# A chunked scan and an expert router: the scan rewritten as masked linear attention on small array tiles

## The chip, the cores and the metric

One core of one Trainium2 chip runs the whole program. The metric is the device time of one execution in microseconds. The kernel before takes 391.32 us, the median of 3 runs (389.31 to 393.22).

## What is computed

For 4 batches and 8 heads of 768 tokens (x has 32 columns, B and C have 16), a state decays by `a` at each token. The output of token i is the sum over earlier tokens j of (C_i . B_j), times the product of the decays between them, times x_j. The reference does it in chunks of 32:

```python
L = np.exp(cum[:, :, :, None] - cum[:, :, None, :]) * causal
y_intra = np.einsum('bhij,bhjd->bhid', np.einsum('bhin,bhjn->bhij', Cc, Bc) * L, xc)
y_inter = np.einsum('bhin,bhnd->bhid', Cc, state) * np.exp(cum)[:, :, :, None]
state = decay_full * state + sum_j(B_j x_j * decay_from_j)
```

The outputs of the 8 heads side by side are 3072 rows of 256. Each row goes to the one expert of 8 whose normalised embedding has the largest cosine with it, and the gate is the softmax weight of that expert:

```python
logits = xn @ en.T / tau
out[mask] = gate_w[mask, None] * (np.maximum(x[mask] @ w1[e], 0) @ w2[e])   # w1 256x1024, w2 1024x256
```

All data is f32. On TensorE a product in f32 shows as two records (two weight loads and two matmuls).

## The kernel before

The scan goes in 24 units: 6 chunks of 128 tokens (`c`) times 4 batches (`b`), all 8 heads of a batch in one unit `u`. `decays` loads `a`, clips it, writes it to a scratch tensor `a_dram` in DRAM and makes the running products `prod` (L96). Per unit, `front` reads the decays of the chunk back from `a_dram`, spread over 128 partitions (`row`), and a scan on VectorE (L158) makes from them the triangular decay matrices `L` of the 8 heads; GpSimd makes `bd`, B scaled by the decay to the chunk's end (L164). `inner` makes the scores `g` of four head groups on four row tiles of the array (L182) and VectorE multiplies each into `L` (L183); `dc` (L186) spreads the decays and `cd` (L188) is C scaled by them. `state` makes the chunk's state (L199), VectorE updates it (L208) and GpSimd masks it into `Sm` (L212). `outputs` adds the state's part (L227) and eight products of `L` and x on four column tiles of the array (L233) into `y`, which ScalarE copies to `yT` (L238). `finish` turns it (L248), makes the router's logits (L250), copies both to `yt` (L253), and squares the row (L255).

After each 4 units `place` picks the expert of each row (VectorE), counts with short bf16 products its slot among the expert's rows (L363), and scatters the rows of `yt` to `rows` in DRAM with four indirect DMAs on GpSimd's queue (L371). Slots that get no row were filled with ones by 8 DMAs on ScalarE's queue (L331).

The experts follow in order: `load` reads 416 rows of an expert as 4 x 104 (L396), `turn_x` turns them (L440), `prepare` makes the gates, `up` and `down` are the two products (L449, L463), and `out` turns back, scales (L479) and scatters four blocks (L480). A loop for rows over 416 of an expert closes the program; it goes round as often as there are such blocks, and starts with a load of that number (L584).

All instructions of an engine are in the order that a scheduler chose from the program's order and its own estimates. Each PSUM tile of the scan has a bank of its own.

Of the kernel before, what the change touches and what calls it, by code (L numbers as in the profile page):

```python
# [8 lines left out]
F32 = mybir.dt.float32  # L9
# [15 lines left out]
CAP = TR * NT  # L25
LEFT = (T - CAP) // Q + E
W = DM + E + 2


class Net:  # L30
    pass

# [5 lines left out]
def build_consts(k):  # L38
    nc, pool = k.nc, k.const
    k.ident = pool.tile([128, 128], F32, name="ident")  # L40
    make_identity(nc, k.ident[:])

    k.diag = k.mc.tile([128, NH, Q], F32, name="diag")
    nc.gpsimd.memset(k.diag[:], 0.0)
    nc.gpsimd.affine_select(
        out=k.diag[:], in_=k.diag[:], pattern=[[0, NH], [-1, Q]], compare_op=ALU.not_equal,
        fill=1.0, base=0, channel_multiplier=1,
    )

    k.spread = k.mc.tile([NB * NH, NB, 128], F32, name="spread")  # L50
    nc.gpsimd.memset(k.spread[:], 0.0)
    nc.gpsimd.affine_select(
        out=k.spread[:].rearrange("k b (q t n) -> k (b q) t n", q=4, t=2),
        in_=k.spread[:].rearrange("k b (q t n) -> k (b q) t n", q=4, t=2),
        pattern=[[-8, NB], [-1, 4], [-4, 2], [0, N]], compare_op=ALU.not_equal,
        fill=1.0, base=0, channel_multiplier=1,
    )

    k.tmask = k.mc.tile([128, 2], F32, name="tmask")
    nc.vector.memset(k.tmask[:], 0.0)  # L60
    same = k.work.tile([128, 128], F32, name="same", tag="sq", bufs=1)
    nc.vector.memset(same[:], 0.0)
    for q in range(4):
        nc.vector.memset(k.tmask[32 * q : 32 * q + N, 0:1], 1.0)
        nc.vector.memset(same[32 * q : 32 * q + 32, 32 * q : 32 * q + 32], 1.0)
    nc.vector.tensor_scalar(
        out=k.tmask[:, 1:2], in0=k.tmask[:, 0:1], scalar1=-1.0, scalar2=1.0, op0=ALU.mult, op1=ALU.add
    )
    k.smask = k.mc.tile([128, 2, 128], F32, name="smask")
    for t in range(2):  # L70
        nc.vector.tensor_scalar_mul(k.smask[:, t, :], same[:], k.tmask[:, t : t + 1])
# [6 lines left out]
def decays(k):  # L78

    nc = k.nc
    a = k.work.tile([NB * NH, S], F32, name="a", tag="L", bufs=3)
    nc.sync.dma_start(a[:], k.a.rearrange("b h s -> (b h) s"))
    nc.vector.tensor_scalar(out=a[:], in0=a[:], scalar1=1e-6, scalar2=1.0, op0=ALU.max, op1=ALU.min)
    head = k.work.tile([NB * NH, S], F32, name="head", tag="L", bufs=3)
    nc.vector.memset(head[:], 0.0)
    nc.vector.tensor_copy(out=head[:, 0:S:Q], in_=a[:, 0:S:Q])
    nc.vector.memset(a[:, 0:S:Q], 0.0)
    for b in range(NB):  # L90
        nc.sync.dma_start(
            k.a_dram[b].rearrange("c h s -> h c s"),
            a[NH * b : NH * b + NH, :].rearrange("h (c s) -> h c s", s=Q),
        )
    k.prod = k.mc.tile([NB * NH, S], F32, name="prod")
    nc.vector.tensor_tensor_scan(  # L96
        out=k.prod[:], data0=a[:], data1=head[:], initial=0.0, op0=ALU.mult, op1=ALU.add
    )
    ps = k.ps.tile([128, NB, NC], F32, name="whole_ps", tag="tp")
    for b in range(NB):  # L100
        nc.tensor.matmul(
            ps[:, b, :], lhsT=k.spread[:, b, :], rhs=k.prod[:, Q - 1 : S : Q], start=True, stop=True
        )
    k.whole = k.mc.tile([128, NB, NC], F32, name="whole")
    nc.vector.tensor_copy(out=k.whole[:], in_=ps[:])


def expert_emb(k):

    nc = k.nc  # L110
    emb = k.work.tile([E, DM], F32, name="emb", tag="emb")
    nc.scalar.dma_start(emb[:], k.emb)
    tau = k.mc.tile([E, 1], F32, name="tau")
    nc.scalar.dma_start(tau[:], k.tau.to_broadcast([E, 1]))
    sq = k.work.tile([E, DM], F32, name="emb_sq", tag="sq", bufs=1)
    r = k.mc.tile([E, 1], F32, name="emb_r")
    nc.scalar.activation(sq[:], emb[:], ACT.Square, accum_out=r[:])
# [4 lines left out]
    nc.vector.tensor_scalar_mul(emb[:], emb[:], r[:])  # L122
    ps = k.ps.tile([128, KD, E], F32, name="emb_ps", tag="tp")
    for j in range(KD):
        nc.tensor.transpose(ps[:, j, :], emb[:, 128 * j : 128 * j + 128], k.ident[:E, :E])
    k.en = k.mc.tile([128, KD, E], F32, name="en")
    nc.vector.tensor_copy(out=k.en[:], in_=ps[:])


def load(k, c):  # L130
    nc = k.nc
    t = Net()
    t.bt = k.inp.tile([128, NB, Q], F32, name="bt", tag="bt")
# [15 lines left out]
def front(k, u):  # L149


# [3 lines left out]
    row = k.work.tile([128, NH * Q], F32, name="row", tag="row")  # L155
# [35 lines left out]
def state(k, u):  # L191
# [4 lines left out]
    if c == NC - 1:  # L196
        return
# [495 lines left out]
```

## Time and profile before

| | us |
|---|---|
| median of 3 runs | 391.32 |
| lowest, highest | 389.31, 393.22 |
| the profiled execution | 392.45 |
| its span, first to last instruction | 390.7 |

| engine | busy us | share of the span |
|---|---|---|
| TensorE, matmuls (PE) | 328.1 | 84% |
| TensorE, weight loads (PEld) | 203.0 | 52% |
| VectorE (DVE) | 179.4 | 46% |
| ScalarE (ACT) | 67.8 | 17% |
| GpSimd (POOL) | 119.1 | 30% |

Busy times are shares of the whole span; the scan and the experts have different limits and are read apart, by stretches of time. A line number such as L233 is the line of the kernel that issued an instruction. A matmul's end is modelled, since matmuls overlap; the distance from one group's start to the next group's start is safer than a busy time.

### The profile page before, as it was taken

What the parts mean: (1) busy time and instruction counts of PE and PEld (TensorE: products, weight loads), DVE (VectorE), ACT (ScalarE), POOL (GpSimd) and SP (SyncE); (2) the same over time, 40 slices, a digit from 0 to 9 for tenths busy, and PEclk for the clock granted to TensorE, in tenths of its full rate; (3) what the DMA queues carried; (4) which work ended last, traced back from release to release, by engine and by line L of the source; (5) the groups of instructions that cost most, each with busy time, mean ns of one, the idle gap of its engine ahead of it and who ended that gap; (6) DMA issues with size and microseconds to landing.
All of it is one profiled execution on the core that took longest, in us unless ns stands there. A gap on an engine that the chain in (4) does not pass through costs nothing. (4 is left out here: it accounts for less than half of the span.)

```text
span 390.7 us, 4519 instructions
## 1 busy us (share of the span) xinstructions
PE 328.1 (84%) x1589; PEld 203.0 (52%) x1589; DVE 179.4 (46%) x460; ACT 67.8 (17%) x195; POOL 119.1 (30%) x147
## 2 busy tenths in 40 slices
PE   2319998699999799607999999999999999999940
PEld 2205566477767576504555555555555555555520
DVE  7137876888897968143314225042241412403020
ACT  1101242142333233200101011011110111101100
POOL 7001444527667562243013014140131401304031
PEclk9999996575868669555999999999999999999995
DMA  7978757487847330125044532445324400101010
GB/s 245 298 273 283 253 173 260 163 271 227 289 153 236 120 117 2 56 87 108 6 146 140 160 106 52 143 142 160 107 68 128 144 3 0 39 0 43 0 34 11
DMA packets 24791, 51.23 MB, mean 131 GB/s; under 512 B 2453, under 2 KB 14175, under 8 KB 24768
## 3 DMA queue, kind: packets, MB, share of 16 engines
q1 hardware_dynamic: 21112, 40.97, 33.0%
q0 software_dynamic: 2688, 6.42, 5.2%
q10 hardware_dynamic: 968, 3.55, 2.6%
q8 instruction: 13, 0.21, 0.2%
q14 instruction: 10, 0.08, 0.1%
HBM read 40.87 MB, written 10.32 MB: 131 GB/s over the span
## 5 line engine op out<-in xcount | busy, mean ns | idle before, releaser
L449 PE MATMUL hp<-xT,w 128*128 128x416 f32 x256 | 97.9, 524 | 0.6 <-DVE xT L441 0.6
L463 PE MATMUL yp<-hT,w 128*128 128x416 f32 x256 | 90.8, 513 | 0.0
L463 PEld LDWEIGHTS yp<-hT,w 128*128 128x128 f32 x256 | 48.1, 190 | 38.5 <-issue 38.5
L449 PEld LDWEIGHTS hp<-xT,w 128*128 128x128 f32 x256 | 47.5, 195 | 33.8 <-issue 32.5
L480 POOL DMA_INDIRECT out_dram<-yo,to x32 | 32.2, 1007 | 103.0 <-DVE yo L479 92.3
L158 DVE TENSOR_TENSOR_SCAN L<-row,diag 128x1024 f32<-128x1024 f32 x24 | 56.2, 2341 | 9.9 <-DMA row<-a_dram 6.2
L182 PE MATMUL g<-ctm,bt 32*128 32x256 f32 x192 | 36.9, 586 | 9.9 <-DVE L L183 9.8
L183 DVE TENSOR_TENSOR L<-g,L 128x256 f32<-128x256 f32 x96 | 35.5, 413 | 17.6 <-POOL bd L164 12.3
L455 DVE TENSOR_SCALAR hT<-hp 128x416 f32<-128x416 f32 x32 | 18.9, 592 | 42.4 <-PE hp L449 28.8
L371 POOL DMA_INDIRECT rows<-yt,row_of x24 | 30.4, 1268 | 19.6 <-issue 14.2
L164 POOL TENSOR_TENSOR bd<-b,L 128x64 f32<-128x64 f32 x48 | 17.4, 384 | 54.3 <-DVE L L158 30.7
L453 ACT ACTIVATE hT<-hp 128x416 f32<-128x416 f32 x32 | 16.6, 517 | 91.7 <-PE hp L449 91.7
L212 POOL TENSOR_TENSOR Sm<-S,smask 128x256 f32<-128x256 f32 x20 | 24.1, 1206 | 18.5 <-DVE S L208 11.2
L417 POOL TENSOR_TENSOR gr<-xg,half 104x4 f32<-104x4 f32 x8 | 8.2, 1030 | 70.2 <-DMA xg<-rows 70.2
L182 PEld LDWEIGHTS g<-ctm,bt 32*128 32x128 f32 x192 | 19.1, 250 | 15.8 <-issue 9.8
L470 DVE COPY yoT<-yp 128x416 f32<-128x416 f32 x8 | 4.7, 591 | 43.8 <-PE yp L463 33.2
L178 ACT ACTIVATE ctm<-ct,tmask 128x128 f32<-128x128 f32 x48 | 16.5, 394 | 44.2 <-PE g L182 25.5
L233 PE MATMUL y<-L,x 128*32 128x128 f32 x384 | 23.9, 366 | 0.0
L199 PE MATMUL st<-x,bd 128*128 128x256 f32 x40 | 20.9, 619 | 1.6 <-DVE S L208 1.6
L186 PE MATMUL dc<-prod,spread 32*128 32x128 f32 x48 | 15.8, 423 | 7.6 <-DVE cd L188 7.5
L479 DVE TENSOR_SCALAR yo<-ot,gate 104x256 f32<-104x256 f32 x32 | 15.3, 480 | 11.2 <-PE ot L477 11.2
L411 DVE TENSOR_REDUCE gm<-xg 104x4 f32<-104x32 f32 x8 | 1.5, 184 | 38.3 <-DMA xg<-rows 38.3
(138 smaller groups left out, 283.0 us busy)
## 6 DMA issues: line engine op xcount, KB each, us to landing
w<-in_moe_w_dram SPq DMA_DIRECT2D x16, 1024.0 KB
row<-a_dram SPq DMA_DIRECT2D x24, 512.0 KB
rows<-none ACTq DMA_DIRECT2D x8, 432.2 KB
xg<-rows SPq DMA_DIRECT2D x8, 432.2 KB
x<-in_x_dram SPq DMA_DIRECT2D x6, 512.0 KB
bt<-in_BT_dram SPq DMA_DIRECT2D x6, 256.0 KB
ct<-in_CT_dram SPq DMA_DIRECT2D x6, 256.0 KB
b<-in_B_dram SPq DMA_DIRECT2D x6, 256.0 KB
```

What stands on the lines that cost most here:

```text
L158: nc.vector.tensor_tensor_scan(out=s.L[:].rearrange("j h i -> j (h i)"), data0=row[:], data1=k.diag[:].rearrange("j h i -> j (h i)"), init ...
L164: nc.gpsimd.tensor_tensor(out=s.bd[:, :, v, :], in0=t.b[:, b, :].rearrange("j (q t n) -> j q t n", q=4, t=2)[:, :, v, :], in1=s.L[:, 4 * v ...
L182: nc.tensor.matmul(g[:], lhsT=t.bt[r, b, :], rhs=ctm[r], start=True, stop=True, tile_position=(32 * q, 0))
L183: nc.vector.tensor_tensor(out=s.L[:, q:NH:4, :], in0=g[:], in1=s.L[:, q:NH:4, :], op=ALU.mult)
L199: nc.tensor.matmul(ps[:], lhsT=s.bd[:].rearrange("j q t n -> j (q t n)"), rhs=t.x[:, b, :], start=True, stop=True)
L212: nc.gpsimd.tensor_tensor(out=k.Sm[u][:].rearrange("p t m -> p (t m)"), in0=new[:], in1=k.smask[:].rearrange("p t m -> p (t m)"), op=ALU.mult,
L233: nc.tensor.matmul(y[32 * q : 32 * q + 32, v, :], lhsT=t.x[:, b, D * h : D * h + D], rhs=s.L[:, h, :], start=(c == 0 and v == 0), stop=Tru ...
L371: d = nc.gpsimd.indirect_dma_start(out=k.rows[:, :], out_offset=bass.IndirectOffsetOnAxis(ap=row[:, b : b + 1], axis=0), in_=k.yt[:, NB * ...
L449: nc.tensor.matmul(t[:], lhsT=s.w1[:, j, 128 * f : 128 * f + 128], rhs=s.xT[:, j, :], start=(j == 0), stop=(j == KD - 1))
L455: nc.vector.tensor_scalar_max(s.hT[:, f, :], t[:], 0.0)
L463: nc.tensor.matmul(t[:], lhsT=s.w2[:, f, 128 * j : 128 * j + 128], rhs=s.hT[:, f, :], start=(f == 0), stop=(f == KF - 1),)
L480: d = nc.gpsimd.indirect_dma_start(out=k.out[:, :], out_offset=bass.IndirectOffsetOnAxis(ap=s.to[:, i : i + 1], axis=0), in_=y[:], in_offs ...
```

## The change

The scan is written anew. The decays are taken relative to the middle of each 64 tokens: with f the product of the decays from there (and its inverse r), a score is (C_i f_i) . (B_j r_j) where i >= j, so B and C are scaled once and the decay matrix becomes a mask of ones and zeros. `load_decays`, `decays`, `turn_decays` and `between` make f, r, the turned r, and the factor from one middle to the next; `a_dram` is gone. C comes from DRAM straight into a zeroed tensor in which the even and odd head of a pair have places of their own (8 loads of 32 KB per chunk instead of one). Per unit there are now 64-token halves: `scale_c` (f spread by a product, then C scaled, then scaled B turned by TensorE and copied), `sums` (the halves' states, 8 products on 64x32 tiles), `inner` (8 products on 32x64 tiles, masked in one step on VectorE), `outputs` (16 products of the states on the four diagonal 32x32 tiles, 16 of the masked scores on 64x32 tiles) and `finish` (two products that turn the output and give the logits together). `states` and `scale_b` run once per chunk on VectorE.

PSUM is now four hand-made tensors: pg (4 banks), py (2 banks, outputs and half states), p6 (turned rows, slots and counts) and p7 (spread f and turned B). TensorE's instructions in the scan keep the order in which the program issues them; the other engines' are still scheduled. `place` is split: `pick` (VectorE) and `place`, two iterations later.

Behind the scan: the rows have 272 columns instead of 266 and lie as two halves with the logits between; the squares move from `finish` to `prepare`; an expert's 416 rows are read as 4 rows in a line per partition; only the last 160 of 416 slots are filled with ones; the experts' SBUF pool is opened after the scan's; an order barrier stands ahead of the closing loop.

```diff
+def decays(k, kk):
+    nc = k.nc
+    tt = nc.vector.tensor_tensor
+    a, f, r = k.a0[:, kk, :], k.f[:, kk, :], k.r[:, kk, :]
+    clip(k, a)
...
+    nc.vector.tensor_tensor_scan(out=f, data0=a, data1=k.heads[:], initial=0.0, op0=ALU.mult, op1=ALU.add)
...
+    nc.vector.reciprocal(out=r, in_=f)
+    for v, s in ((r, w[:, 0, :]), (f, w[:, 1, :])):
+        v = v.rearrange("p (h s) -> p h s", h=2)[:, :, 0:SQ]
+        tt(out=v, in0=v, in1=s.unsqueeze(2).to_broadcast([128, 2, SQ]), op=ALU.mult)
+
+def between(k):
...
+    nc.vector.memset(one[:, SQ:S:HQ], 1.0)
+    p = k.mc.tile([NB * NH, S], F32, name="p")
+    nc.vector.tensor_tensor_scan(out=p[:], data0=a[:], data1=one[:], initial=0.0, op0=ALU.mult, op1=ALU.add)
+    k.g = k.mc.tile([NB * NH, NK - 1], F32, name="g")
+    nc.vector.tensor_tensor(out=k.g[:], in0=p[:, HQ + SQ - 1 : S : HQ], in1=at[:, 1:], op=ALU.mult)
+
 def load(k, c):
...
+    t.ct = k.ctz[c % 3]
+    for i in range(8):
+        q, v = divmod(i, 2)
+        r = slice(32 * q + N * v, 32 * q + N * v + N)
+        (nc.scalar if c == 0 and i % 2 else nc.sync).dma_start(
+            t.ct[r, v].rearrange("p b m -> p (b m)"), k.CT[c][r]
+        )
...
+def sums(k, u):
...
+        for q in range(4):
+            nc.tensor.matmul(
+                k.py[32 * q : 32 * q + 32, h, 256 + 64 * b : 320 + 64 * b], lhsT=t.bp[r, b, 32 * q : 32 * q + 32],
+                rhs=t.x[r, b, :].rearrange("p (t q d) -> p q t d", t=2, q=4)[:, q],
+                start=True, stop=True, tile_position=(HQ * h, 32 * q),
+            )
+
+def states(k, c):
+    nc = k.nc
+    for h in range(2):
+        i = (2 * c + h)
+        if i > 0:
+            k.T[i] = k.stp.tile([128, NB, 64], F32, name="T", tag="T", bufs=6)
+            nc.vector.tensor_tensor(
+                out=k.T[i][:], in0=k.V[:], in1=k.whole[:, :, i - 1 : i].to_broadcast([128, NB, 64]), op=ALU.mult
+            )
...
+            nc.vector.tensor_tensor(out=k.V[:], in0=k.T[i][:], in1=s, op=ALU.add)
+
+def scale_c(k, u):
...
+    f = k.p7[:, 128 * (u % 2) : 128 * (u % 2) + 128]
+    nc.tensor.matmul(
+        f, lhsT=k.spread[g : g + 32, b, :], rhs=k.f[g : g + 32, c // 4, :], start=True, stop=True,
+        tile_position=(g, 0),
+    )
+    s.cp = k.work.tile([128, 2, Q], F32, name="cp", tag="cp", bufs=4)
+    nc.vector.tensor_tensor(
+        out=s.cp[:], in0=t.ct[:, :, b, :], in1=f.unsqueeze(1).to_broadcast([128, 2, Q]), op=ALU.mult
+    )
+    bt = k.p7[:, 256 + 128 * (u % 2) : 384 + 128 * (u % 2)]
+    nc.tensor.transpose(bt, t.bp[:, b, :], k.ident[:])
+    s.bt = k.work.tile([128, Q], F32, name="bt", tag="bt", bufs=3)
+    nc.scalar.copy(out=s.bt[:], in_=bt)
 
 def inner(k, u):
...
+    a = 128 * (u % 4)
+    for q in range(4):
+        for h in range(2):
+            r, m = slice(32 * q, 32 * q + 32), slice(HQ * h, HQ * h + HQ)
+            nc.tensor.matmul(
+                k.pg[m, q, a : a + 128], lhsT=s.bt[r, m], rhs=s.cp[r, :, m], start=True, stop=True,
+                tile_position=(32 * q, HQ * h),
+            )
+    s.g = k.work.tile([128, 4, 2, HQ], F32, name="g", tag="g", bufs=3)
+    nc.vector.tensor_tensor(
+        out=s.g[:], in0=k.pg[:, :, a : a + 128].rearrange("p q (t i) -> p q t i", t=2),
+        in1=k.mask[:].unsqueeze(1).unsqueeze(1).to_broadcast([128, 4, 2, HQ]), op=ALU.mult,
+    )
 
 def outputs(k, u):
...
+            for q in range(4):
+                r = slice(32 * q, 32 * q + 32)
+                nc.tensor.matmul(
+                    at(q, h, v), lhsT=T[r, b, 32 * v : 32 * v + 32], rhs=s.cp[r, v, HQ * h : HQ * h + HQ],
+                    start=(v == 0), stop=False, tile_position=(32 * q, 32 * q), skip_group_check=True,
+                )
     for v in range(2):
         for q in range(4):
...
+            for h in range(2):
+                r = slice(HQ * h, HQ * h + HQ)
+                n = 32 * (4 * v + q)
+                nc.tensor.matmul(
+                    at(q, h, v), lhsT=t.x[r, b, n : n + 32], rhs=s.g[r, q, v, :],
+                    start=((2 * c + h) == 0 and v == 0), stop=True, tile_position=(HQ * h, 32 * q),
+                    skip_group_check=True,
+                )
...
 def finish(k, u):
...
+    for j, at in ((0, 0), (1, LG)):
         nc.tensor.matmul(
+            k.p6[:, at : at + Y1], lhsT=yT[:, j].rearrange("p h i -> p (h i)"), rhs=k.turn[:, j, :],
+            start=(j == 0), stop=(j == 1), skip_group_check=True,
+        )
+    nc.scalar.copy(out=k.yt[:, u, 0:TOK], in_=k.p6[:, 0:TOK])
 
 def mamba(k):
...
+    scale_b(k, 0)
+    between(k)
+    for i in range(NU + 3):
+        c, b = divmod(i, NB)
+        if b == 0 and c + 2 < NC:
+            load(k, c + 2)
+        if i in (8, 14, 20):
+            load_weights(k, (i - 8) // 6)
+        if i < NU:
+            scale_c(k, i)
+        if i == 0:
+            spread_between(k)
+            for v in range(NB):
+                sums(k, v)
+        elif NB <= i + 3 < NU:
+            sums(k, i + 3)
...
+        if b == 0 and c < NC:
+            states(k, c)
+            if c + 1 < NC:
+                scale_b(k, c + 1)
+        if 0 <= i - 1 < NU:
+            inner(k, i - 1)
+        if 0 <= i - 2 < NU:
+            outputs(k, i - 2)
+        if 0 <= i - 3 < NU:
+            finish(k, i - 3)
+        if b == 2 and c > 0:
+            pick(k, c - 1)
+        if b == 0 and c > 1:
+            place(k, c - 2)
+    place(k, NC - 1)
...
     def load(s, e):
...
+            s.x[:].rearrange("p t w -> p (t w)"),
+            s.k.rows[T * e : T * e + CAP, :].rearrange("(p t) w -> p (t w)", t=s.nt),
...
     def prepare(s, has):
...
+        for i in range(nt):
+            sq = k.p.tile([tr, 2, 128], F32, name="sq", tag="sq")
+            nc.scalar.activation(
+                sq[:], s.x[:, i, :].rearrange("p (j w) -> p j w", j=KD)[:, :, 0:128], ACT.Square,
+                accum_out=r[:, i : i + 1],
+            )
...
 def leftover(k):
...
+    k.tc.no_sync_barrier()
     blocks = nc.values_load(table[0:1, 1, 0:1], min_val=0, max_val=LEFT)
```

In this, HQ is 64, NK is 12 (the halves), Y1 is 136 and TOK is 264.

## Rows read from the trace of the kernel before

**Rows 1.** The page: the granted clock of PE in 40 slices, tenths.

```profile
PEclk9999996575868669555999999999999999999995
```

**Rows 2.** Busy time by stretch; columns: engines' busy us (records), PEclk, DMA share, GB/s.

```profile
30.00:165.00 135.00, 122.28 (x911) 88.14 (x909) 102.91 (x205) 41.65 (x138) 66.79 (x86) 0.76 0.56 186
...
62.60:83.10 20.50, 17.39 (x107) 12.89 (x107) 14.74 (x23) 4.34 (x14) 10.20 (x12) 0.51 0.63 205
...
205.00:245.00 40.00, 40.00 (x137) 22.10 (x136) 13.88 (x39) 4.87 (x10) 9.14 (x9) 1.00 0.39 120
```

**Rows 3.** Groups by line and shape: busy us, mean ns, idle before and its releaser.

```profile
L158 DVE TENSOR_TENSOR_SCAN L<-row,diag 128x1024 f32<-128x1024 f32 x24 | 56.2, 2341 | 9.9 <-DMA row<-a_dram 6.2 <-PE y L233 3.7
L183 DVE TENSOR_TENSOR L<-g,L 128x256 f32<-128x256 f32 x96 | 35.5, 413 | 17.6 <-POOL bd L164 12.3 <-PE g L182 5.0
L96 DVE TENSOR_TENSOR_SCAN prod<-a,head 32x768 f32<-32x768 f32 x1 | 2.2, 2208 | 0.0
```

**Rows 4.** Tile y: ns of one (least, median, most), first and last start.

```profile
L233 PE MATMUL y<-L,x x384: 272/421/423, 32.6 to 159.5; 128*32 128x128 f32 x192
```

**Rows 5.** PE in order of time, early and late: start us, us, group.

```profile
32.59 1.08 PE L233 MATMUL y<-L,x 128*32 128x128 f32 x16
...
158.79 1.08 PE L233 MATMUL y<-L,x 128*32 128x128 f32 x16
159.81 0.69 PE L248 MATMUL tp<-ident,yT 128*128 128x128 f32 x2
160.29 0.86 PE L250 MATMUL tp<-en,yT 128*128 128x8 f32 x4
```

**Rows 6.** PE in order of time, around 100 us.

```profile
96.39 1.22 PE L199 MATMUL st<-x,bd 128*128 128x256 f32 x2
97.40 1.06 PE L227 MATMUL y<-cd,Sm 128*128 128x128 f32 x4
98.39 1.08 PE L233 MATMUL y<-L,x 128*32 128x128 f32 x16
...
102.54 0.64 PE L233 MATMUL y<-L,x 128*32 128x128 f32 x16
103.11 0.44 PE L248 MATMUL tp<-ident,yT 128*128 128x128 f32 x2
```

**Rows 7.** All engines in order of time: a product, its read, the next.

```profile
12.81 0.79 PE L186 MATMUL dc<-prod,spread 32*128 32x128 f32 x2 [0.38 <-DVE cd L188]
...
13.64 0.29 DVE L188 TENSOR_TENSOR cd<-dc,ct 128x128 f32<-128x128 f32 x1 [0.88 <-PE dc L186]
13.99 0.49 PEld L186 LDWEIGHTS dc<-prod,spread 32*128 32x128 f32 x2 [0.68 <-DVE cd L188]
```

**Rows 8.** The scan's start on DVE, and ACT's longest wait up to 20 us.

```profile
25.86 2.29 DVE L158 TENSOR_TENSOR_SCAN L<-row,diag 128x1024 f32<-128x1024 f32 x1 [4.83 <-DMA row<-a_dram]
28.82 1.42 DVE L183 TENSOR_TENSOR L<-g,L 128x256 f32<-128x256 f32 x4 [0.68 <-POOL bd L164]
...
ACT ctm L178 <- DMA rows<-none: 13.7, 1, 13.7
```

**Rows 9.** The scan's end: last copy of yt, then the slots' records.

```profile
163.37 0.38 ACT L253 COPY yt<-tp 128x264 f32<-128x264 f32 x1 [1.43 <-PE tp L250]
...
164.92 0.18 PE L363 MATMUL at<-ob,before_b 128*128 128x32 bf16 x1 [1.58 <-DVE ob L350]
...
165.19 0.17 PE L382 MATMUL n_ps<-sums,ones_b 128*128 128x8 bf16 x1
```

**Rows 10.** The reload: its issue on SP, first reader, first up-product.

```profile
173.19 6.74 SPq L396 DMA_DIRECT2D xg<-rows  x3
177.83 0.19 DVE L411 TENSOR_REDUCE gm<-xg 104x4 f32<-104x32 f32 x1 [6.55 <-DMA xg<-rows]
...
180.18 13.88 PE L449 MATMUL hp<-xT,w 128*128 128x416 f32 x32 [0.62 <-DVE xT L441]
```

**Rows 11.** The last two scatters, and the closing chain's wait for one.

```profile
378.71 1.00 POOL L480 DMA_INDIRECT out_dram<-yo,to  x1 [0.30 <-POOLq L584]
384.25 1.00 POOL L480 DMA_INDIRECT out_dram<-yo,to  x1 [4.54 <-issue]
...
378.71 3.58 DMA out_dram<-yo,to
```

More of the change, by code (lines that the diff above doesn't have):

```diff
@@ L59, in build_consts @@
[L59 to L68, printed above, removed]
@@ L75, in build_consts, with load_decays @@
     k.yt = pool.tile([128, NU, W], F32, name="yt")
-def decays(k):
+    nc.gpsimd.memset(k.yt[:, :, TOK:], 0.0)
+def load_decays(k):
     nc = k.nc
[L83 to L93, printed above, removed]
-        )
[L95 to L99, printed above, removed]
+    k.a0 = k.mc.tile([128, 2, Q], F32, name="a0")
+    nc.vector.memset(k.a0[64:128, 1, :], 1.0)
+    a = k.a.rearrange("b h s -> (b h) s")
+    for c in range(NC):
+        (nc.sync if c % 2 else nc.scalar).dma_start(
+            k.a0[32 * (c % 4) : 32 * (c % 4) + 32, c // 4, :], a[:, Q * c : Q * c + Q]
+        )
+    k.a1 = k.mc.tile([NB * NH, S], F32, name="a1")
+    nc.scalar.dma_start(k.a1[:], a)
@@ L230, in outputs @@
     for v in range(2):
         for q in range(4):
-            h = 4 * v + q
-            nc.tensor.matmul(
-                y[32 * q : 32 * q + 32, v, :], lhsT=t.x[:, b, D * h : D * h + D], rhs=s.L[:, h, :],
-                start=(c == 0 and v == 0), stop=True, tile_position=(0, 32 * q), skip_group_check=True,
-            )
-    s.yT = k.work.tile([128, KD, Q], F32, name="yT", tag="yT")
-    nc.scalar.copy(out=s.yT[:], in_=y[:])
+            for h in range(2):
+                r = slice(HQ * h, HQ * h + HQ)
+                n = 32 * (4 * v + q)
[4 more added lines that the diff above has]
+                )
@@ L258, in mamba @@
+    nc.scalar.copy(out=k.yt[:, u, 0:TOK], in_=k.p6[:, 0:TOK])
 def mamba(k):
[L259 removed]
+    k.f = k.mc.tile([128, 2, Q], F32, name="f")
+    k.r = k.mc.tile([128, 2, Q], F32, name="r")
+    k.rT = k.mc.tile([128, 2, 128], F32, name="rT")
+    k.V = k.mc.tile([128, NB, 64], F32, name="V")
+    k.T = {}
+    load_decays(k)
     load(k, 0)
+    decays(k, 0)
+    turn_decays(k, 0)
     load(k, 1)
     expert_emb(k)
[L263 to L282 removed]
+    scale_b(k, 0)
@@ L365, in place @@
         )
-    nc.vector.tensor_tensor(out=oh[:], in0=at[:], in1=ob[:], op=ALU.mult)
+    if c == NC - 1:
+        n = k.p6[:, 304 : 304 + E]
+        for i in range(NC):
+            nc.tensor.matmul(n, lhsT=k.ones[:], rhs=k.sums[:, i, :], start=(i == 0), stop=(i == NC - 1))
+    oh = w.tile([128, NB, E], F32, name="oh", tag="oh")
+    nc.vector.tensor_tensor(out=oh[:], in0=at, in1=ob[:], op=ALU.mult)
+    m = w.tile([128, NB], F32, name="m", tag="m")
     nc.vector.reduce_sum(out=m[:], in_=oh[:], axis=AX.X)
```

357 lines of the change are left out of this document (181 added, 176 removed).

## The prediction

> **What bounds the kernel now.** I read the page's shares and clock row first, then the busy time by stretch, then the groups of the scan, then the order of time around its start, its end and the kernel's end. The span has three parts. The experts, from 180 us on, keep PE busy at full clock without a hole [rows 2]; the diff leaves their products alone. The scan runs from 29 us, when the first product of scores and decays can start [rows 8], to 163.4 us, when the copy of the last turned unit starts [rows 9]; that is 134 us for 24 units, 5.6 us each. Between and behind lie a scatter with a reload (163 to 180) and a tail.
>
> In the scan PE is busy 122 of 135 us and DVE 103 [rows 2]. DVE has a scan of 2.34 us a unit, four products of 0.41 and smaller work [rows 3], over 5 us with the state and the routing; PE fills as much, because its clock is mostly 1.2 GHz: y<-L records have a median of 421 ns, where they take 272 at full clock [rows 4]. (The clock row reads 9 up to 55 us [rows 1], yet the y<-L group at 32.59 us took the 1.08 us of the half clock [rows 5]; I trust the group.) So PE and DVE bind together, and what is saved on DVE alone is worth little.
>
> **What the change takes away and what is left.** The broadcast decays, their scans, the four products, `bd` and `Sm` go. DVE has then per unit one 256-wide product for `cp` (0.41 by L183 [rows 3]) and one 512-wide for `g` (about 0.75), and per 128 tokens four for the states, two for `scale_b` and the routing: about 2.2 us a unit in all. ACT has three copies, about 1.0 us, POOL one scatter. None of them can bind; PE must, and the sum is a sum over PE.
>
> **PE per unit.** A product in f32 is two records. The y<-L group (16 records on four column tiles, so four passes of 128 columns each) takes 1.02 us to the next group at half clock [rows 5] and 0.57 at full [rows 6]. Twice the difference, 0.90, is columns: 0.225 us per pass of 128. The 0.12 left is the price of leaving one array form for the next. PE's new fixed order has six forms per unit. I take passes on different tiles as concurrent, as those four are, and cost as proportional to columns:
> - `f`, then the wait for `cp`, then the turn of B'. They share one PSUM tensor p7 and `cp` reads between. The old chain dc, cd, dc has that shape: 1.18 us with a read of 0.29 [rows 7]; with 0.41 it is 1.30.
> - turn of B': half of L248's 0.48 [rows 5], 0.24.
> - `sums`: 16 records on 8 tiles, two passes of 64: 0.23.
> - `inner`: two passes of 128: 0.45.
> - states times C': 32 records on the 4 diagonal tiles, eight passes of 64: 0.90.
> - `g` times x: 32 records on 8 tiles, four passes of 64: 0.45.
> - turn with logits: 4 records of 136 columns: 0.96.
> - six forms at 0.12: 0.72.
>
> Together 5.25 us. That is nearly the old 5.6: the records per unit rise from 38 (8 + 2 + 2 + 4 + 16 + 2 + 4 by the lines L182 to L250) to 103 (2 + 1 + 16 + 16 + 64 + 4), and most of the saved work was DVE's.
>
> Whether the turn of B' waits for `cp` no row shows, since no two tiles share a bank before. Bounds: 0.77 for f alone and 1.30; I take 1.30, the row of like shape. The Trainium skill (PSUM — Partial Sum Buffer, PSUM bank collisions raise a hardware error) says that TensorE may not write a bank while another engine reads it, other columns included. By that the wait must be there and the sum stays; without it a unit would be 0.53 us shorter.
>
> Whether 64 columns cost half of 128 no row shows either. Bounds: half, or the same 0.225, which adds 1.58 us a unit. The nearest row of narrow products is the routing's: ten records of 32 columns or fewer in 0.27 us, 27 ns each [rows 9]. That is nearer the low end, so I take half.
>
> **The clock.** I take 1.2 GHz throughout. A busy PE alone does not raise it: from 62.6 to 83.1 us PE was busy 17.4 of 20.5 us and the clock read 0.51 [rows 2]. It rose near 100 us behind st, y<-cd and y<-L, all using the array's whole width, back to back [rows 6]. The change puts smaller tiles and a wait per unit in their place.
>
> **Per 128 tokens.** The slots (`place`) share the bank of the turn, so PE waits for the copy of yt: drain 0.2, copy 0.38, then 15 short records at 27 ns [rows 9], about 1.05 us. The states read the two banks that the outputs write: three dependent DVE steps of 0.41 behind `sums`, less the `inner` that runs meanwhile (0.57), about 0.95. Five times 2.0 is 10 us.
>
> **Start.** The a_dram round trip (L158 waited for a row until 25.86, and ACT 13.7 us behind the fills [rows 8]) is gone. PE's first turn now needs `g` of `between` on DVE: the decays' load (about 4 us), the constants (2.5), `decays` (1.8, small steps), `scale_b` (0.8) and `between` (3.8, of which its 768-long scan is 2.2 by the old one of prod [rows 3]). That is 12 to 13 us, then eight records and `sums` of four units, 2 us: the first turn ends at 15. Bounds 12 and 20; the latter if ACT's eight fills (174 KB each, 432 before) still hold up its copies of B'.
>
> **Sum.** Turn 1 lacks outputs and finish (2.5), turn 2 finish (4.1), 21 full turns are 110.3, the extras 10, and three turns drain the pipeline: 4.5, 2.8 and 1.8. 15 + 2.5 + 4.1 + 110.3 + 10 + 9.1 = 151 against 163.4: 12 us. Behind it the same six routing steps and four scatters follow. The reload took 4.64 us from 173.19 with pieces of 1064 bytes [rows 10]; in pieces of 4352 bytes I give it 1.0 us, bounds 0 and 2. The squares of four rows (about 0.6 each) now stand ahead of the first gate on ACT: they end about when the first up-product does, and only the output needs them.
>
> At the end, the last of four scatters starts at 384.25, behind the skipped loop, though the third was at 378.71 [rows 11]. The order barrier puts it in front: it starts at 380.0, and the wait for its landing (3.6, as now for the third [rows 11]) and the closing steps follow. Of the 5.5 us between the two, 4 are gained; bounds 2 and 5. Total 12 + 1 + 4 = 17. The profiled execution took 392.45 us (span 390.7), 1.1 above the median: 392.45 - 17 = 375.4, or 374.5 against the median. I say **375**.
>
> **Rivals.**
> - *A floor per record.* If no record starts under 27 ns behind the last, as in the routing's rows [rows 9], the 32 records of `g` times x take 0.86 instead of 0.45 and the 16 of `sums` 0.43 instead of 0.23; the others keep their passes. A unit is 5.86, 14 us more in all: 389, no change. For it: no row shows sustained starts closer; y<-L's are 36 ns apart at full clock [rows 6]. Against it: there columns explain the 36. The Trainium skill (TensorE: Matmul & The Clock Gate, Wait — 56ns, not 53.3ns?) gives a floor of about 25 ns from start to start. By that figure the case would be 387.
> - *Narrow tiles no cheaper (the other side).* If 64 columns cost the pass of 128, a unit is 6.83 and the scan 36 us longer: 411. Break-even is 0.7 us more than my 5.25, so it decides from a 64-column pass of 0.16 us on. Against it stand the 27 ns. The Trainium skill (TensorEngine Tiling (Array Packing), Instruction Overhead) warns that a product costs about 60 cycles however narrow, and not to tile a dimension that is already small. At 64 columns and two cycles each that alone changes nothing here.
> - *Full clock.* If PE reaches 2.4 GHz in the scan, the columns halve (3.23 to 1.61) and f with its wait falls to about 0.95: 3.28 a unit, 45 us less: 330. Against it is the stretch at 0.51.
> - *No wait on p7*: 4.72 a unit, 12 us less: 363. It lies in the range of the first case.
>
> **How the numbers follow.** The forecast, with no floor and half clock, holds 0.60 (own range 358 to 388); the floor 0.16; narrow tiles no cheaper, or not concurrent, 0.14; full clock 0.10. The range leaves out most of full clock below and half of the narrow case above: 350 to 405. About 1% is what a measurement can tell from no change. Faster by that: nearly all of the first and the full clock, 0.68; same, most of the floor case and a rim of the first, 0.12; slower 0.20.
>
> **What would show it.** Right: PE's records at half clock throughout the scan; turns of about 5.25 us with one hole of 0.5 behind `f`; DVE under half busy; the last turn near 151 us; all four last scatters before the loop. Wrong: a clock of 1.0 in the scan; holes behind ACT or DVE elsewhere; records of `g` times x at an even 27 ns or more; a first turn later than 20 us.

## The result, and the profile after

The forecast was 375 us, and the changed kernel took 375.11 us in the first comparison. It took the same on chip 3. On chip 14 it gained nothing at all, which no step of the prediction foresaw. The chip of the first comparison is not on record. All times are medians, with the lowest and highest in brackets, and the ratio to the kernel before on the same occasion with its 95% interval. The ratios leave out executions more than 1.5% above the fastest of the same kernel; the medians don't.

| occasion | kernel before, us | changed kernel, us | ratio |
|---|---|---|---|
| first comparison | 391.49 (389.31 to 393.22) | 375.11 (373.69 to 378.19) | 0.9595 [0.9512, 0.9677] |
| chip 7 | 391.23 (388.15 to 393.76) | not run there | |
| chip 3 | 392.78 (388.91 to 393.80) | 375.45 (373.57 to 376.27) | 0.9570 [0.9519, 0.9622] |
| chip 14 | 391.41 (390.22 to 393.60) | 392.29 (389.49 to 394.67) | 1.0017 [0.9987, 1.0047] |

The kernel before takes 391 to 393 us everywhere. The profile after is of an execution of the first comparison that took 378.19 us (span 376.5), 3.1 us above its median. From the page, the shares of the engines and the clock:

```profile
PE 318.4 (85%) x3079; PEld 191.5 (51%) x3079; DVE 123.5 (33%) x383; ACT 62.6 (17%) x189; POOL 76.3 (20%) x90
...
PEclk9999999975555556758999999999999999999995
```

Busy time by stretch (engines' busy us and records, PEclk, DMA share, GB/s):

```profile
30.00:165.00 135.00, 105.45 (x2154) 72.37 (x2153) 44.55 (x140) 22.24 (x65) 23.45 (x24) 0.71 0.30 98
...
85.00:145.00 60.00, 53.02 (x1041) 36.63 (x1033) 18.66 (x53) 10.55 (x31) 11.18 (x12) 0.50 0.12 39
```

DVE's 102.91 us between 30 and 165 [rows 2] have become 44.55, while PE runs 2154 records there instead of 911 and is busy 105 us: PE alone binds, at half clock. A turn is one round of the loop over the units, from its product f to the next f; the turn of B' is the transposition in it. One turn, PE in order of time:

```profile
64.64 0.79 PE L266 MATMUL p<-f,spread 32*128 32x128 f32 x2
65.94 0.48 PE L275 MATMUL p<-ident,bp 128*128 128x128 f32 x1 [0.52 <-DVE cp L271]
66.35 0.47 PE L232 MATMUL py<-x,bp 64*32 64x64 f32 x16
66.75 0.73 PE L288 MATMUL pg<-cp,bt 32*64 32x128 f32 x16
67.41 1.08 PE L316 MATMUL py<-cp,T 32*32 32x64 f32 x32
68.41 0.68 PE L325 MATMUL py<-g,x 64*32 64x64 f32 x32
69.02 1.27 PE L341 MATMUL p<-turn,yT 128*128 128x136 f32 x4
70.22 0.79 PE L266 MATMUL p<-f,spread 32*128 32x128 f32 x2
```

A turn takes 5.58 us, forecast 5.25, with the one hole that was forecast. The clock row still reads 9 here, as it does up to 55 us in the kernel before [rows 1]; the groups last as long as they do at 99 to 107 us, where it reads 0.50, so this too is half clock. In the runs below I also take the clock from the length of the groups where the row reads 9 ahead of its first change. Where a chunk of 128 tokens begins, the states' wait and the wait of `place`:

```profile
102.83 1.08 PE L316 MATMUL py<-cp,T 32*32 32x64 f32 x32 [0.91 <-DVE V L255]
...
106.19 0.19 PE L492 MATMUL p<-ob,before_b 128*128 128x32 bf16 x1 [0.47 <-ACT yt L345]
```

The start: ACT's second copy of B', behind its fills, and PE's second f, where the first turn ends (forecast 15):

```profile
18.39 0.27 ACT L277 COPY bt<-p 128x128 f32<-128x128 f32 x1 [5.05 <-DMA rows<-none]
```

```profile
15.89 0.79 PE L266 MATMUL p<-f,spread 32*128 32x128 f32 x2
```

The scan's end, the reload and the first up-product, where [rows 9, 10] stood at 163.37, 173.19, 177.83 and 180.18:

```profile
151.88 0.38 ACT L345 COPY yt<-p 128x264 f32<-128x264 f32 x1 [0.82 <-PE p L341]
...
159.49 0.96 POOL L506 DMA_INDIRECT rows<-yt,row_of  x1 [0.30 <-issue]
...
162.45 6.35 SPq L534 DMA_DIRECT2D xg<-rows  x3
...
166.69 0.19 DVE L553 TENSOR_REDUCE gm<-xg 104x4 f32<-104x32 f32 x1 [7.88 <-DMA xg<-rows]
...
168.41 1.06 PE L595 MATMUL hp<-xT,w 128*128 128x416 f32 x1
```

Of the 14.2 us between the two spans (390.7 and 376.5), 11.5 are there when the scan ends and 11.8 at the first up-product; the experts give 0.9 more, and the end 1.5.

### The profile page after: what moved, and what is told of

Same layout as the page of the kernel before. It is cut to its first block, busy times and chain, and to the rows that moved or that the text cites. A ratio compares the mean times of both kernels' runs of the same rounds, so it can differ in the third digit from the quotient of the medians.

```text
span 376.5 us, 7301 instructions
## 1 busy us (share of the span) xinstructions
PE 318.4 (85%) x3079; PEld 191.5 (51%) x3079; DVE 123.5 (33%) x383; ACT 62.6 (17%) x189; POOL 76.3 (20%) x90
## 4 chain that ended last, share of the span: by engine, by line
PE 71%; DMA 11%; issue 7%; DVE 5%; SPq 1%; POOL 1%; ACT 1%; ACTq 0%; DVEq 0%; POOLq 0%
PE hp L595 20%; PE yp L609 18%; PE p L341 7%; DMA out_dram<-yo,to 7%; PE py L316 6%; PE p L266 4%; PE py L325 4%; PE pg L288 3%; PE p L275 3%; DVE cp L271 3%; PE py L232 2%; PE ot L623 2%; PE xt L586 2%; DMA x<-in_x_dram 1%; DMA xg<-rows 1%
## 5 line engine op out<-in xcount | busy, mean ns | idle before, releaser
L601 DVE TENSOR_SCALAR hT<-hp 128x416 f32<-128x416 f32 x32 | 18.9, 591 | 40.3 <-PE hp L595 38.0
L341 PE MATMUL p<-turn,yT 128*128 128x136 f32 x96 | 29.0, 454 | 0.5 <-ACT yt L345 0.5
L316 PE MATMUL py<-cp,T 32*32 32x64 f32 x704 | 23.5, 302 | 3.9 <-DVE V L255 3.9
L271 DVE TENSOR_TENSOR cp<-ctz,p 128x256 f32<-128x256 f32 x24 | 10.1, 420 | 45.6 <-PE p L266 43.0
L341 PEld LDWEIGHTS p<-turn,yT 128*128 128x128 f32 x96 | 21.7, 308 | 4.5 <-issue 3.8
L316 PEld LDWEIGHTS py<-cp,T 32*32 32x32 f32 x704 | 17.8, 157 | 11.6 <-DVE V L255 5.7
L275 PE MATMUL p<-ident,bp 128*128 128x128 f32 x24 | 11.2, 468 | 14.7 <-DVE cp L271 14.7
L293 DVE TENSOR_TENSOR g<-pg,mask 128x512 f32<-128x512 f32 x24 | 16.5, 688 | 21.2 <-PE pg L288 21.1
L625 DVE TENSOR_SCALAR yo<-ot,gate 104x256 f32<-104x256 f32 x32 | 15.4, 480 | 11.5 <-PE ot L623 11.5
L266 PE MATMUL p<-f,spread 32*128 32x128 f32 x48 | 18.7, 490 | 0.4 <-ACT rT L123 0.4
L331 ACT COPY yT<-py 128x256 f32<-128x256 f32 x24 | 8.9, 372 | 59.4 <-PE py L325 59.4
L288 PE MATMUL pg<-cp,bt 32*64 32x128 f32 x384 | 17.2, 436 | 0.0
```

The lines of the kernel that those rows point to most:

```text
L266: nc.tensor.matmul(f, lhsT=k.spread[g : g + 32, b, :], rhs=k.f[g : g + 32, c // 4, :], start=True, stop=True, tile_position=(g, 0),)
L271: nc.vector.tensor_tensor(out=s.cp[:], in0=t.ct[:, :, b, :], in1=f.unsqueeze(1).to_broadcast([128, 2, Q]), op=ALU.mult)
L275: nc.tensor.transpose(bt, t.bp[:, b, :], k.ident[:])
L288: nc.tensor.matmul(k.pg[m, q, a : a + 128], lhsT=s.bt[r, m], rhs=s.cp[r, :, m], start=True, stop=True, tile_position=(32 * q, HQ * h),)
L293: nc.vector.tensor_tensor(out=s.g[:], in0=k.pg[:, :, a : a + 128].rearrange("p q (t i) -> p q t i", t=2), in1=k.mask[:].unsqueeze(1).unsqu ...
L316: nc.tensor.matmul(at(q, h, v), lhsT=T[r, b, 32 * v : 32 * v + 32], rhs=s.cp[r, v, HQ * h : HQ * h + HQ], start=(v == 0), stop=False, tile ...
```

## The experiments

**The end: without the order barrier, and without the loop** (both on chip 7; the function `leftover` holds both, so the second edit takes out the barrier too)

```diff
 def leftover(k):
-    k.tc.no_sync_barrier()
```
```diff
         moe(k)
-        leftover(k)
```

> The order barrier ahead of the closing loop is taken out again; all else is the changed kernel. As predicted before the run: 4 us longer (379), the last of the four scatters behind the loop. By the traces (the tail from the last turn back's start to the end is 16.65 us before and 15.15 after): 1.5 us longer (376.6), since GpSimd's closing drain takes 4.65 us in the changed kernel and 5.90 before, and covers most of the late scatter.

> The closing loop for rows over 416 of an expert is left out (with this data it goes round no time, so the output is whole). If GpSimd's closing drain of 4.65 us waits for the scatters, it gets longer by what the loop's checks took (about 3 us from 367.3 to 371.0) and the time stays within 1 us of 375. If the drain has a price of its own, the time falls by about 3 us, to 372.

The first of the last four scatters and the last one, GpSimd in order of time; changed kernel, without barrier, without loop (spans 376.5, 388.8, 389.5):

```profile
363.40 1.00 POOL L626 DMA_INDIRECT out_dram<-yo,to  x1 [16.19 <-DVE yo L625]
...
367.32 1.00 POOL L626 DMA_INDIRECT out_dram<-yo,to  x1 [0.30 <-issue]
```
```profile
375.18 1.00 POOL L626 DMA_INDIRECT out_dram<-yo,to  x1 [16.20 <-DVE yo L625]
...
382.34 1.00 POOL L626 DMA_INDIRECT out_dram<-yo,to  x1 [3.56 <-issue]
```
```profile
378.78 1.00 POOL L626 DMA_INDIRECT out_dram<-yo,to  x1 [16.20 <-DVE yo L625]
...
382.70 1.00 POOL L626 DMA_INDIRECT out_dram<-yo,to  x1 [0.30 <-issue]
```

From the first of the four to the end of the span: 13.1 us in the changed kernel, 13.6 without the barrier, 10.7 without the loop, 14.6 before (its first of the four starts at 376.10). So the barrier does put the last scatter in front, by 3.2 us, and that is worth 0.5. Without barrier and loop the end comes 2.4 us sooner than in the changed kernel, with the four scatters as close together (first to last 3.92 us in both): the loop's own instructions and what GpSimd closes behind them set the end there. Another 1.0 of the 1.5 gained came with a part of the change that these runs don't single out.

As whole kernels these two disagreed with everything expected (376.6 or 379 us for the first, 372 or 375 for the second): 389.75 us (386.62 to 394.16), 0.9948 [0.9898, 0.9998], and 387.69 us (383.85 to 391.25), 0.9889 [0.9845, 0.9933]. Against the first comparison 13 to 15 us are lost, and they lie in the scan, which the edits don't touch: in the two traces the last scatter of token rows starts 12.1 and 16.2 us later (171.56 and 175.64, against 159.49). Why they are lost is the question that led the rest of the runs.

**The hole behind f: moved, and filled** (chip 7)

The turn of B' goes behind the inner products of the turn before:

```diff
+def turn_b(k, u):
+    nc = k.nc
+    c, b = divmod(u, NB)
+    t, s = k.ld[c], k.un[u]
     bt = k.p7[:, 256 + 128 * (u % 2) : 384 + 128 * (u % 2)]
     nc.tensor.transpose(bt, t.bp[:, b, :], k.ident[:])
...
         if 0 <= i - 1 < NU:
             inner(k, i - 1)
+        if i < NU:
+            turn_b(k, i)
```

> The turn of B' (L275 of the changed kernel) is issued behind the next unit's sums and inner instead of straight behind f, so PE has 0.40 + 0.66 us of other work while VectorE makes cp. Theory: PE alone binds the scan, and the 0.51 us hole behind f is time on its path. Then the hole goes in 23 turns: 12 us less than the changed kernel (375 to about 363), turns of 5.07 us, records at 1.2 GHz as before. Rival 1: the turn and its copy are then late for the next f, which shares the bank, and the hole only moves: within 2 us of 375. Rival 2: with the hole gone PE is denser and the clock rises in part of the scan: under 355.

It took 372.18 us (367.25 to 376.41), 0.9421 [0.9331, 0.9512]. A turn in order of time:

```profile
43.77 0.79 PE L266 MATMUL p<-f,spread 32*128 32x128 f32 x2
44.49 0.47 PE L232 MATMUL py<-x,bp 64*32 64x64 f32 x16
...
48.77 0.58 PE L266 MATMUL p<-f,spread 32*128 32x128 f32 x1
```

The hole is gone and the turn is 5.00 us. This is the proof of the wait on p7: the same records cost 0.58 us less when the turn of B' isn't due while DVE reads the bank. The groups keep their half-clock lengths in these turns, and the clock rose only at 145 us. The whole kernel missed the expected 363 us: its 14th and 18th turns, beside the scatters, took 7.24 and 7.29 us, and the changed kernel wasn't run on this chip to compare with.

The other edit leaves the order and puts four idle bf16 products into the hole:

```diff
+    for i in range(4):
+        nc.tensor.matmul(k.p6[:, 384:512], lhsT=k.ones[:], rhs=k.ones[:], start=True, stop=True, skip_group_check=True)
     bt = k.p7[:, 256 + 128 * (u % 2) : 384 + 128 * (u % 2)]
```

> Four idle bf16 products of 128 columns into spare columns of p6 stand in the hole between f and the turn of B'; the rest is the changed kernel. They compute nothing that is used. Theory that only the hole's place on PE's path counts: they need at most 4 x 0.107 us at half clock, fit the hole of 0.51, and the time stays within 3 us of 375. Rival: the clock follows from how densely the array is used, and the filled hole lifts it to 2.4 GHz in part of the scan: turns of about 3.3 us there, and 360 or less, down to 330 if it holds throughout.

```profile
46.21 0.79 PE L266 MATMUL p<-f,spread 32*128 32x128 f32 x2
46.94 0.61 PE L275 MATMUL p<-ones_b 128*128 128x128 bf16 x4
47.52 0.47 PE L277 MATMUL p<-ident,bp 128*128 128x128 f32 x1
```

389.68 us (385.13 to 392.37), 0.9916 [0.9867, 0.9964]. The turns stay at 5.58 us and at half clock up to 78 us, with the hole filled. And here as in the two kernels of the end, one turn in four was long, most of them 7.5 to 9.7 us.

**Does the chip make the long turns, or the edit?** The unaltered kernel beside altered ones, on chip 3 and on chip 14, with the barrier taken out once more on the latter.

> The changed kernel, unaltered, beside three others on one chip. In the runs with the hole filled, without the order barrier and without the last loop, one turn in four took 7.5 to 9.6 us instead of 5.6 (the turn that runs while GpSimd issues the four scatters of a chunk), 14 us in all, although TensorE's instructions in the scan were those of the changed kernel. Theory A: the long turns come with the chip or the occasion, and not with the edits. Then the changed kernel shows them too in this run: four turns of 7.5 to 9.6 us, about 388 us, and the three edits cost and gain nothing by themselves. Rival B: the long turns come with the edits. Then the changed kernel has no turn over 7.4 us again, and takes 374 to 378 us.

> The changed kernel, unaltered, once more beside three altered ones on one chip, because the long turns were seen in one call (without this kernel in it) and not in the next. Theory A, that they come with the chip or the occasion: whatever happens, this kernel and the one without the order barrier, whose TensorE instructions in the scan are the same, behave alike: both with turns of 5.2 to 7.4 us and 374 to 378 us, or both with four turns of 7.5 to 9.6 us and 385 to 391 us. Rival B, that they come with the edits: this one takes 374 to 378 us and the one without the barrier 386 to 391 us.

> The order barrier ahead of the last loop taken out, once more, beside the unaltered kernel. Theory A: within 1.5 us of the unaltered kernel, of which the end of the kernel costs 0.5 us (from the first of the last four scatters to the end 13.6 us here and 13.1 us there), and no more long turns than that one has. Rival B: 11 to 15 us slower than the unaltered kernel of this call, by turns of 7.5 to 9.6 us behind place.

Turns behind `place`, from the start of f to the next, by the order of time of each trace:

| kernel, chip | us | turn 10 | turn 14 | turn 18 | turn 22 |
|---|---|---|---|---|---|
| changed, first comparison | 375.11 | 5.58 | 5.58 | 5.55 | 5.19 |
| changed, chip 3 | 375.45 | 5.58 | 5.58 | 5.55 | 5.19 |
| without barrier, chip 7 | 389.75 | 7.55 | 9.62 | 9.53 | 9.36 |
| changed, chip 14 | 392.29 | 8.32 | 9.83 | 9.69 | 9.65 |
| without barrier, chip 14 | 392.72 | 8.32 | 9.87 | 9.69 | 9.65 |

On chip 14 the two kernels are alike (without the barrier 1.0012 [0.9979, 1.0044] to the kernel before). Theory A holds: the edit is not the cause, the chip or the occasion is. Each chip was used on one occasion only, so these two are not told apart; "on chip 14" below means both. The four turns are 15.6 us longer there, which is most of the 18.9 between the spans 371.7 and 390.6. The rest isn't singled out; the clock was full at other times, too (135.6 to 149.3 us on chip 3; 72.8 to 79.6 and from 161.5 us on chip 14). Turn 14, PE in order of time, chip 3 and then chip 14:

```profile
85.86 1.08 PE L316 MATMUL py<-cp,T 32*32 32x64 f32 x32
86.86 0.68 PE L325 MATMUL py<-g,x 64*32 64x64 f32 x32
87.47 1.27 PE L341 MATMUL p<-turn,yT 128*128 128x136 f32 x4
```
```profile
85.98 1.32 PE L316 MATMUL py<-cp,T 32*32 32x64 f32 x27
87.61 0.44 PE L316 MATMUL py<-cp,T 32*32 32x64 f32 x5 [0.32 <-issue]
87.98 0.82 PE L325 MATMUL py<-g,x 64*32 64x64 f32 x5
89.81 0.45 PE L325 MATMUL py<-g,x 64*32 64x64 f32 x5 [1.01 <-issue]
91.24 0.68 PE L325 MATMUL py<-g,x 64*32 64x64 f32 x22 [0.97 <-issue]
91.84 1.27 PE L341 MATMUL p<-turn,yT 128*128 128x136 f32 x4
```

The same instructions at the same place: on chip 14 they come in pieces, some of five records, with up to a microsecond between, and nothing that the profile shows is waited for ("issue"). The waits of PE from 62 to 165 us, chip 14, add up to:

```profile
PE py L325 <- issue: 7.2, 16, 1.0
```

There is no such line for chip 3. Other engines are late too; "remote" is a release that the profile can't put down to any instruction. On chip 14, g of that turn on DVE, then the first and the last of GpSimd's four scatters:

```profile
87.65 0.69 DVE L293 TENSOR_TENSOR g<-pg,mask 128x512 f32<-128x512 f32 x1 [2.89 <-remote]
```
```profile
85.53 0.96 POOL L506 DMA_INDIRECT rows<-yt,row_of  x1 [19.00 <-ACT bt L277]
...
89.32 0.96 POOL L506 DMA_INDIRECT rows<-yt,row_of  x1 [0.30 <-issue]
```

On chip 3 that g started at 86.03, with the inner products ahead of it only 0.12 us earlier than here. With the turn of B' moved, a run that comes below, ACT and DVE wait 6 us on chip 14 beside four scatters (79.71 to 84.47), and PE waits for ACT:

```profile
85.58 0.37 ACT L338 COPY yT<-py 128x256 f32<-128x256 f32 x1 [6.14 <-remote]
```

The long turns lie where the scatters run; the next two kernels ask whether they are the cause.

**Scatters held back, scatters spread**

```diff
     for b in range(NB):
-        d = nc.gpsimd.indirect_dma_start(
...
+        k.due.append((c, b, row, m))
...
     place(k, NC - 1)
+    while k.due:
+        scatter(k)
```

> The changed kernel with all scatters of the token rows held until the scan is over (24 behind the last place, instead of 4 behind each), which makes it slower behind the scan: 20 more scatters at the 1.25 us from start to start that they show, 25 us. What is read here is the scan. Theory S: TensorE's turns are long where GpSimd's four scatters run beside them. Then all turns from the sixth on take 5.2 to 5.6 us, those with the states of a chunk 6.1 to 6.5 and those that place follows 6.3 to 7.4, and the 24th turn starts at 140 us or earlier. Rival I: the turns are long because TensorE's instructions arrive late at this point of the program, whatever GpSimd does. Then turns of 7.5 to 9.6 us stay where they were, and the 24th starts at 150 to 155 us.

It took 376.02 us (373.29 to 376.25) on chip 3 and tells nothing about scatters: the scheduler put them back beside the scan (from 61.5 us on, each within 3 us of its place in the changed kernel on this chip). It is the changed kernel once more, without long turns on that chip.

The next one makes the order a matter of data: row numbers are made by an operation that reads the g of the turn. It also has the turn of B' behind the inner products.

```diff
+        nc.vector.scalar_tensor_tensor(
+            out=row[:, b : b + 1], in0=after, scalar=0.0, in1=m[:, b : b + 1], op0=ALU.mult, op1=ALU.add
+        )
...
+        if k.due and i - 1 < NU:
+            scatter(k, k.un[i - 1].g[:, 0, 0, 0:1])
```

> The version with the turn of B' behind the inner products, and with the four scatters of a chunk spread, one behind the g of each of the next four turns (its row numbers are made by an operation that reads that g). By theory S, if four scatters one behind the other are what holds TensorE up, the turns of 7.2 to 7.5 us that this version showed go back to 5.0 to 6.3, four of them or some 8 us, and it takes 360 to 366 us. If each scatter costs its own share wherever it stands, every turn becomes 5.5 to 6 us instead of four long ones, and it takes 367 to 375 us as without the spreading. If scatters have nothing to do with it, the long turns stay at the same places: 367 to 376 us.

> The turn of B' behind the inner products, with the scatters as they are, once more. Turns of 5.0 us where nothing else holds them, 0.58 us less than the unaltered kernel's, 19 turns: 11 us, and more where the granted clock rises for want of the wait: 355 to 365 us where the unaltered kernel takes 375 us. If the long turns show in this call they stand in it as well: 367 to 376 us.

> The same with the scatters spread over the turns, beside the kernel without the spreading in the same call. Theory S, that four scatters behind each other hold TensorE up: this one has no turn over 6.5 us whether the other has them or not, and is 8 us or more faster than the other if it has them. Rival: the spreading does nothing, and the two are within 3 us of each other; then what brought 354 us in the call before was the turn of B' and the clock that it met.

On chip 3 it took 353.53 us (341.57 to 365.88; too far apart for a ratio). On chip 14, in one comparison: with the turn moved alone 374.46 us (369.59 to 377.47), 0.9484 [0.9418, 0.9549]; with the scatters spread as well 361.59 us (360.66 to 371.49), 0.9214 [0.9183, 0.9245]. The moved turn alone is 17.8 us under the changed kernel of this comparison, both together are 31 us under it: the best version of the study, on the chip where the changed kernel gained nothing. What one and two scatters do, on chip 14, PE and then GpSimd:

```profile
75.35 0.83 PE L332 MATMUL py<-g,x 64*32 64x64 f32 x19
76.48 0.45 PE L332 MATMUL py<-g,x 64*32 64x64 f32 x6 [0.30 <-issue]
77.24 0.47 PE L332 MATMUL py<-g,x 64*32 64x64 f32 x7 [0.31 <-issue]
...
78.85 0.58 PE L266 MATMUL p<-f,spread 32*128 32x128 f32 x1
```
```profile
74.46 0.96 POOL L500 DMA_INDIRECT rows<-yt,row_of  x1 [8.56 <-DVE row_of L497]
75.76 0.96 POOL L500 DMA_INDIRECT rows<-yt,row_of  x1 [0.34 <-issue]
82.45 0.96 POOL L500 DMA_INDIRECT rows<-yt,row_of  x1 [5.73 <-DVE row_of L497]
```

The first two scatters of a chunk still run behind each other, and their turn (72.16 to 78.85) takes 6.69 us. The third runs alone, and its turn (78.85 to 83.85) takes 5.00, as without any. The next chunk repeats it: 6.65 us for its pair (95.21 to 101.86), 4.97 for the turn with one. On chip 3 the same kernel's pair costs nothing (its 14th turn takes 5.00). So, on chip 14, a lone scatter costs nothing, a pair 1.7 us, and four in a row 4.1 to 4.5 us in the changed kernel's last three of these turns (9.83, 9.69, 9.65 less 5.58, 5.55, 5.19). Theory S is borne out by the turns, with two of them a little over the 6.5 us that it allowed. Of what lies between the two kernels, 10.6 us by their ratios, not all is shown to be the scatters', since the clock also was full at other times (72.8 to 83.0 and 144.5 to 151.3 us in the one, 43.3 to 56.9, 111.5 to 121.8 and 128.6 to 135.4 in the other).

**The order left to the scheduler** (chip 3)

```diff
-        with tc.manual_schedule(engines={PE}):
-            build_consts(k)
-            route_consts(k)
-            mamba(k)
+        build_consts(k)
+        route_consts(k)
+        mamba(k)
```

> One part of the change undone: TensorE's order in the scan is the scheduler's and not that of the program. The products are the same. Its order puts the turns of B' between and behind the inner products, puts states and g times x in other places, and lets the logits of one turn stand beside the f of the next. If the fixed order is worth something, it is the wait for cp and the place of the states: 0.5 us a turn either way, so 363 to 390 us by my reckoning. If the fixed order carries the gain, it takes 390 us or more; if the order doesn't matter, the time is that of the unaltered kernel in this call, within 4 us.

```profile
41.09 0.79 PE L266 MATMUL p<-f,spread 32*128 32x128 f32 x2
...
42.20 0.69 PE L288 MATMUL pg<-cp,bt 32*64 32x128 f32 x4
42.82 0.47 PE L275 MATMUL p<-ident,bp 128*128 128x128 f32 x1
43.23 0.72 PE L288 MATMUL pg<-cp,bt 32*64 32x128 f32 x12
...
52.76 0.34 PE L232 MATMUL py<-x,bp 64*32 64x64 f32 x16
```

367.63 us (362.00 to 376.61), 0.9287 [0.9201, 0.9374], 7.8 less than with the fixed order on this chip. Its turn at half clock is the same, 5.61 us (41.09 to 46.70): no hole, but the turn of B' splits the inner products in two. It is ahead mostly because the clock was full from 52.4 to 69.5 us, where a turn takes 3.3 to 3.8: turns 9 to 12 take 14.0 us, 24.1 in the fixed order on this chip, and that is 10.0 of the 11.8 us by which its scan ends sooner in the two traces. Whether its order brought the clock is not shown. The unaltered kernel's clock first rose at 75.9, 135.6 and 72.8 us in its three traces. And with the turn of B' moved, TensorE's order is the same in three traces up to the first scatters (57 us in two, 53 in the third): with the scatters as they are it ran at half clock to 145.5 us on chip 7 and to 72.8 on chip 14, and with the scatters spread it was at full clock from 43.3 us on chip 14, as this f shows (0.48 us where 0.79 is half clock):

```profile
43.48 0.48 PE L266 MATMUL p<-f,spread 32*128 32x128 f32 x2
```

So the fixed order is not what the gain comes from.

## Why the prediction was right, and where it wasn't

**The scan's bound and the columns: right.** Per turn, from start to start, measured against forecast: f and its wait 1.30 (1.30), turn of B' 0.41 (0.36), sums 0.40 (0.35), inner 0.66 (0.57), states 1.00 (1.02), g times x 0.61 (0.57), turn with logits 1.20 (1.08), each with its 0.12 for the form. The order of the sizes is that of the columns, and the 0.33 missing is spread over the smaller forms: with the columns at their forecast price, 0.10 to 0.24 is left at each change of form, not 0.12 throughout.

**The wait on p7: right**, 0.52 us of hole, and 0.58 a turn when it is avoided. It was priced from a chain of like shape [rows 7] and came out to the hundredth. That is also what the Trainium skill says (PSUM — Partial Sum Buffer, PSUM bank collisions raise a hardware error): no write of TensorE to a bank while another engine reads it, other columns included. The trace agrees in so far as the program waits; no run here wrote without waiting.

**The floor and the dear narrow tile: fallen.** The 32 records of g times x start within 0.61 us, 19 ns each, under the 27 of the routing's rows [rows 9]. The Trainium skill (TensorE: Matmul & The Clock Gate, Wait — 56ns, not 53.3ns?) gives a floor of about 25 ns, and that section does not speak of tiles; the 19 ns, on eight array tiles, lie below it. With narrow tiles no cheaper a turn would take 6.83.

**The clock: right for most of the scan in the first comparison**, half from 85 to 145 us, full for 3.4 us from 75.9 and from 147.6 to the scan's end. A clock of 1.0 in the scan stood among the signs of being wrong, and those 7.7 us are one. They are worth about 3 of the scan's 11.5 us at most (0.8 in the turn at 75.8 and, if all of it is the clock, 2.35 in the drain); the version with the scatters spread had about 24 us at full clock by 122 us on chip 14. When it rises is not settled: one kernel's first rise differs from trace to trace by up to 73 us (72.8 and 145.5 with the turn moved).

**The sum: right by terms that cancel.** The first full turn begins at 23.73 instead of 21.6 (+2.1): the first turn ends 0.9 late, and the second takes 3.9 instead of 2.5, with 0.72 in it for turning the router's embeddings (L179), which the sum had left out. ACT's copy of B' did wait 5.05 us behind the fills, the bound named for it, but the products that read that copy start at 21.88 without a wait, so it cost nothing. The 20 turns from there to the last f cost 0.33 more each (+6.6). The extras of a chunk came to 5.8 instead of 10 (-4.2): the states alone cost 0.55 once, states and `place` together 0.8 to 1.8. About 0.8 of the 4.2 is the clock, since one of these turns met it at full (6.55 us, 7.33 on chip 3). Three turns with less work were 1.2 shorter, and the drain took 12.0 instead of 14.35, at full clock from 147.6 (-2.35). Together +0.95: 151.9, forecast 151. So that the scan ended where it was forecast is luck, with turns 6% too long and extras 42% too short. Over the whole kernel the profiled execution gained 11.5 in the scan, 0.3 up to the first up-product, 0.9 in the experts (not forecast, and its cause is open) and 1.5 at the end, 14.2 where 12 + 1 + 4 = 17 was forecast: it took 378.19 us, and that the median of the comparison is 375.11 is luck, too.

**The reload: mis-sized.** From issue to first reader it takes 4.24 us instead of 4.64, but it is issued 2.96 us behind the last scatter instead of 2.49. Of the 1.0 us nothing is left at the first reader.

**The end: the step that failed.** I let the kernel end a fixed time after its last scatter's landing. It ends 9.2 us after the start of that scatter, before 6.45 [rows 11]: the loop, and what follows it on GpSimd, set the end. The barrier brought 0.5 of the 4 us, the whole end 1.5.

**What was missing altogether** is that GpSimd's four scatters can hold up TensorE. No rival named it, and the trace of before doesn't show it. On chip 14 the longer turns take 15.6 us, nearly the whole gain. That the forecast time was met rests also on the chips of the first comparison and chip 3. Why the kernel before, which issues its scatters four in a row too, doesn't lose there, and what differs between the chips or the occasions, is open: no trace of before on chip 7 or 14 was at hand.

## What to carry to other kernels

Cost many small array tiles by columns, and add something for each change of form (0.10 to 0.24 us at half clock was left here), and move a write out of the PSUM bank that another engine is reading. Don't let indirect DMAs follow each other beside a stream of short TensorE instructions: tie each to data of its own turn, since the scheduler here put scatters that were only issued later back beside the scan. It paid on chip 14; what such a scatter costs on another chip has to be measured there. And measure a small gain on more than one chip before it is believed.

## What the runs showed that was not expected

On chips 7 and 14, and not on chip 3, TensorE, and with it DVE and ACT, started late without a wait that the profile names while four scatters of 0.96 us each ran: pieces up to 1 us apart, on chip 14 7.2 us in 16 gaps. The scatters themselves take 0.96 us on either kind of chip. That instructions arrive late is what this looks like, but no run shows it; the instruction queue moved the same 0.41 MB in 25 packets on chips 3 and 14.

The clock stayed at 1.2 GHz through a TensorE without holes (two turns of 5.00 from 38.8 to 48.8 us), and was at 2.4 GHz from 43.3 us in another trace with the same order of the products up to there. What made the difference is open.

The skipped closing loop and its barrier put 2.4 us on the end of the kernel (13.1 us from the first of the last four scatters, 10.7 without them); the loop without the barrier put 2.9.
